# A fused attention and feed-forward kernel: maxima over partitions on TensorE, another order for the first units, less elementwise work on GpSimd

## The chip, the cores and the metric

The kernel runs on one core of one Trainium2 chip. The metric is device time in microseconds (us), as the median of several executions; lower is better.

## The reference

```python
scores = q @ k.T / sqrt(64)                      # batch 8, heads 8, sequence 576, head size 64
mask   = 0 <= rel < 32                           # heads 0 to 3: a plain window
         0 <= rel < 128 and rel % 4 == 0         # heads 4 to 7: a dilated window
attn   = softmax(where(mask, scores, -1e9))
x      = (attn @ v), heads side by side          # 4608 tokens x 512
h      = x @ w_in                                # 512 x 2048
g      = h * tanh(softplus(h))                   # Mish
out    = g @ w_out                               # 2048 x 512
```

q, k and v are float32. The two weight matrices are float64 (they come to the chip as 64-bit words), and the output is float32.

## The kernel before

The 4608 tokens are cut into 16 units of 288 tokens, two for each batch element. A unit goes through these steps, and the program names them by two letters: `ld` and `lv` load q, k and v; `pr` finds the largest magnitudes and makes power-of-two scales; `sc` computes a head's scores on TensorE and reduces them on DVE (VectorE); `ex` takes the exponential on ACT (ScalarE); `tp` transposes the probabilities; `va` multiplies by the values and normalises; `tx` transposes a pair of heads to x and splits it into a high and a low float16 half; `ff` is one of 16 blocks of the first product (twelve matmuls, L603) with Mish on ACT (L608); `gt` splits the result into two halves (ACT L623, then DVE L625, or POOL for the pairs in `ON_POOL`; POOL is GpSimd); `fo` is one of 16 blocks of the second product (L635), whose output is scaled (L642) and stored. A name such as `ff1.8` is unit 1, block 8; `sc0.7` is unit 0, head 7; `fo1.2.3` is unit 1, output block 2, part 3.

A feed-forward of one unit is 384 matmuls of 128 x 128 by 288 float16 columns: three products stand for one in higher precision, so each weight and each x is kept as a high and a low half. The first four units (`DIRECT`) compute attention in float32 straight from the loaded tensors. Units 4 to 15 split q, k, v and the probabilities in float16 halves and transpose the probabilities by DMA.

The weights are prepared on the chip while the first units run. There are two matrices (k = 0, 1), four column groups (g) and two parts (p), so 16 parts of 1 MB. A part goes through `wl` (load), `wm` (largest magnitude on DVE, L168, and a copy on ACT, L204), `ws` (the scale of a group, over both parts), `ww` (the float64 words turned into a float32, on DVE, L246, L247 and in some cases L249) and `wp` (scaled and split into two float16 halves). How a part is split is in the table `WAYS`: the first letter says whether the scaling is done through a sign and scale word on DVE (L260) with a product on POOL (L265), "S", or by ACT (L262), "A"; the second whether the low half is subtracted on POOL ("P") or DVE ("D") (L269). ACT makes the high half (L267).

The scale needs a maximum over the 128 partitions. That is `partition_all_reduce` on POOL: L210 for the eight weight groups, L336 for the 16 units.

For the first units the order of all instructions on every engine is written out in `ORDER`, a list of step names. A step is a generator; each time its name stands in the list it runs on to its next `yield`, so a step's pieces on different engines stand at different places. `kw` are matmuls on zeros. Engines run their own queues in this order, and SP (SyncE) issues all loads and stores in it. The list of before ends with the feed-forwards of units 0 and 1, attention of units 0 to 2 and the scores and exponentials of unit 3. What follows is sorted by due times (`at`, `heads`; 32 slots a unit), which fix TensorE's order alone. Loaded tensors share the tag `ld` with five buffers, raw weights have four buffers.

Softmax for heads in `BIASED` subtracts the maximum inside the exponential on ACT, one instruction for each block (L467); the others subtract on DVE (L452) and take one exponential.

Of the kernel before, what the change touches and what calls it, by code (L numbers as in the profile page):

```python
# [42 lines left out]
wp0.0.0 va0.3 sc1.0 kw5 va0.4 wm0.1.1 tx0.1 va0.5 ws0.1 wp0.0.0 va0.4 wl0.2.1 tx0.1 ww0.1.1 tp0.6 va0.5 tp0.6 ws0.1
wl0.2.0 va0.4 tx0.1 kw16 kw9 va0.6 va0.5 tp0.7 va0.6 ws0.1 tp0.7 tx0.2 sc1.2 va0.6 tx0.2 wp0.1.0 wp0.1.1 va0.7 sc1.6
tx0.2 wp0.1.0 fs0.1 sc1.4 sc1.2 va0.7 va0.7 wp0.1.1 kw4 sc1.5 wp0.1.0 sc1.6 tx0.3 tx0.3 sc1.4 kw4 sc1.1 wp0.1.0 tx0.3
kw2 sc1.3 sc1.5 ff0.0 sc1.1 wl0.3.1 ff0.3 ff0.0 sc1.3 lv1 wm0.2.0 ff0.1 ff0.3 wm0.2.1 wm0.2.0 ff0.4 lv2 ws0.2 ff0.1
ws0.2 ww0.2.0 wm0.2.1 ff0.6 ff0.4 ff0.5 ww0.2.1 ff0.6 wl0.3.0 ff0.2 ff0.5 ff0.7 ff0.2 wm0.3.1 gt0.0 sc1.7 ws0.2
# [728 lines left out]
```

## Time and profile before

| | |
|---|---|
| median of 3 runs | 1001.24 us (1000.7 to 1001.33) |
| the profiled execution: its own time | 1003.94 us |
| its span, first to last instruction | 1002.2 us |
| mean granted TensorE clock | 0.949 |
| TensorE busy, VectorE busy | 939.1 us, 674.8 us |
| ScalarE busy, GpSimd busy | 499.4 us, 86.0 us |

An engine's busy time is the sum of its instructions. The granted clock is the share of full speed that the clock of TensorE was given: at half of it a matmul takes twice as long. Most groups of instructions are given by line, engine, operation and the names of the tiles, with their count, busy time and mean duration in ns; behind the last bar stands how long the engine had been idle just before them and what ended that idle time.

### The profile page before, as it was taken

What the parts mean: (1) busy time and instruction counts of PE and PEld (TensorE: products, weight loads), DVE (VectorE), ACT (ScalarE), POOL (GpSimd) and SP (SyncE); (2) the same over time, 40 slices, a digit from 0 to 9 for tenths busy, and PEclk for the clock granted to TensorE, in tenths of its full rate; (3) what the DMA queues carried; (4) which work ended last, traced back from release to release, by engine and by line L of the source; (5) the groups of instructions that cost most, each with busy time, mean ns of one, the idle gap of its engine ahead of it and who ended that gap; (6) DMA issues with size and microseconds to landing.
All of it is one profiled execution on the core that took longest, in us unless ns stands there. A gap on an engine that the chain in (4) does not pass through costs nothing.

```text
span 1002.2 us, 21764 instructions
## 1 busy us (share of the span) xinstructions
PE 939.1 (94%) x8826; PEld 765.1 (76%) x8826; DVE 674.8 (67%) x1417; ACT 499.4 (50%) x926; POOL 86.0 (9%) x142
## 2 busy tenths in 40 slices
...
POOL 1320217142000000000000000000000000000000
PEclk6758597989999999999999999999999999999999
...
GB/s 278 29 115 105 121 96 84 219 12 97 146 129 155 81 145 67 157 35 173 49 159 75 136 87 115 126 88 140 67 174 52 113 13 141 8 56 20 18 7 24
DMA packets 138757, 98.02 MB, mean 98 GB/s; under 512 B 96033, under 2 KB 125345, under 8 KB 138657
## 3 DMA queue, kind: packets, MB, share of 16 engines
...
q8 instruction: 69, 1.13, 0.5%
q14 instruction: 32, 0.25, 0.1%
...
## 4 chain that ended last, share of the span: by engine, by line
PE 70%; DVE 13%; issue 6%; DMA 5%; POOL 2%; SPq 2%; ACT 2%; DVEq 0%; ACTq 0%; POOLq 0%
PE ph L603 31%; PE po L635 29%; DMA pT<-p 4%; PE psc L436 3%; PE pav L542 3%; PE psc L430 1%; PE px L568 1%; DVE raw L247 1%; DVE raw L260 1%; PE pav L536 1%; DVE am L168 1%; DVE m L168 1%; DVE nm L450 1%; DVE g L625 1%; DVE sb L452 1%
## 5 line engine op out<-in xcount | busy, mean ns | idle before, releaser
L603 PE MATMUL ph<-x,w 128*128 128x288 f16 x3072 | 408.4, 288 | 2.7 <-ACT w L204 1.1
L635 PE MATMUL po<-g,w 128*128 128x288 f16 x3072 | 393.3, 288 | 5.8 <-POOL w L269 5.8
L635 PEld LDWEIGHTS <-w 128*128 128x128 f16 x3072 | 297.7, 98 | 81.3 <-POOL w L269 6.0
L603 PEld LDWEIGHTS <-w 128*128 128x128 f16 x3072 | 295.2, 99 | 76.6 <-DVE w L246 2.0
L608 ACT ACTIVATE hm<-ph,fs 128x288 f32<-128x288 f32 x256 | 127.4, 499 | 219.0 <-PE ph L603 218.6
L625 DVE SCALAR_TENSOR_TENSOR g<-hm,sg,g 128x1152 f16<-128x1152 f32 x61 | 87.9, 1441 | 42.4 <-ACT g L623 42.4
...
L508 DVE TENSOR_TENSOR p<-sb,p 96x352 f16<-96x352 f32 (+3 forms) x96 | 48.4, 524 | 55.5 <-ACT p L506 55.4
L623 ACT ACTIVATE g<-hm,sg 128x1152 f16<-128x1152 f32 x61 | 76.3, 1251 | 0.6
L642 DVE TENSOR_SCALAR y<-po,fo 128x288 f32<-128x288 f32 x64 | 32.7, 511 | 48.0 <-PE po L635 47.6
L556 DVE TENSOR_TENSOR xs<-pav,rec 96x192 f32<-96x192 f32 (+1 forms) x128 | 49.4, 386 | 11.1 <-PE ptp L515 0.5
L452 DVE TENSOR_TENSOR sb<-sb,nm 96x256 f32<-96x256 f32 (+3 forms) x120 | 52.4, 449 | 1.1
L450 DVE TENSOR_REDUCE nm<-sb 96x2 f32<-96x256 f32 (+3 forms) x120 | 51.0, 441 | 1.2
L436 PE MATMUL psc<-ks,qs 128*96 128x128 f16 (+3 forms) x672 | 47.0, 211 | 4.9 <-DVE sb L444 2.8
L473 ACT ACTIVATE sb<-sb,ln_p 96x352 f32<-96x352 f32 (+3 forms) x96 | 49.1, 581 | 0.1
L436 PEld LDWEIGHTS <-qs 128*72 128x72 f16 (+1 forms) x672 | 42.7, 119 | 7.0 <-issue 5.2
L542 PEld LDWEIGHTS <-pT 128*128 128x128 f16 (+3 forms) x1008 | 43.1, 98 | 5.8 <-issue 1.4
L582 DVE TENSOR_TENSOR x<-px,x 128x288 f16<-128x288 f32 x48 | 30.0, 625 | 16.0 <-ACT x L580 16.0
L168 DVE TENSOR_REDUCE m<-vn 128x1 f32<-128x768 f32 x16 | 15.2, 949 | 32.3 <-DMA vn<-in_v 23.9
L515 PE MATMUL ptp<-ident,sb 96*128 96x96 f32 (+3 forms) x112 | 15.4, 273 | 19.8 <-ACT sb L472 16.6
L444 DVE SCALAR_TENSOR_TENSOR sb<-psc,sc,m_g 96x384 f32<-96x384 f32 (+1 forms) x48 | 29.7, 619 | 4.2 <-PE psc L436 4.2
L568 PE MATMUL px<-ident,xs 72*128 72x72 f32 (+1 forms) x224 | 28.4, 245 | 3.7 <-DVE xs L556 3.5
...
## 6 DMA issues: line engine op xcount, KB each, us to landing
...
```

The lines of the kernel that those rows point to most:

```text
L436: nc.tensor.matmul(pt[:nq, col:col + nk], d["qs"][:, h, pair, q0:q0 + nq], d["ks"][i][:, h, k0:k0 + nk], start=(i == 0), stop=(i == 1))
L450: nc.vector.tensor_reduce(nm[:nq, j:j + n], x, axis=AX.X, op=ALU.max, negate=True)
L452: nc.vector.tensor_tensor(o, x, nm[:nq, j:j + n].unsqueeze(2).broadcast_to([nq, n, w]), op=ALU.add)
L473: return [nc.scalar.activation(x, x, AF.Exp, bias=ln_p[:nq])]
L508: nc.vector.tensor_tensor(lo, src, hi, op=ALU.subtract)
L542: nc.tensor.matmul(avv[:, j], pp[:nk, c:c + P], vv[vi][:nk, j, head % 4, :], start=(i == 0), stop=(i == 2))
L556: nc.vector.tensor_tensor(xs[:nq, :nb, (head % 2) * D:(head % 2 + 1) * D], avv[:, :, :D], rc.unsqueeze(2).broadcast_to([nq, nb, D]), op=AL ...
L603: nc.tensor.matmul(ph[:, :HT], w1[:, c, j, wi, k * P:(k + 1) * P], d["x"][xi][:, c, :], start=(n == 0), stop=(n == len(seq) - 1))
L608: in_turn("mish", [nc.scalar.activation(d["m"][j][:, k], ph[:, :HT], AF.Mish, scale=d["fs"][:, j:j + 1])])
L623: nc.scalar.activation(g[:, 0], m, AF.Identity, scale=sg)
L625: nc.vector.scalar_tensor_tensor(g[:, 1], m, sg, g[:, 0], ALU.mult, ALU.subtract)
L635: nc.tensor.matmul(po[:, :HT], w2[:, e, j, wi, k * P:(k + 1) * P], d["g"][j][:, gi, k, :], start=(j == 0 and n == 0), stop=(j == NCH - 1 a ...
```

## The change

1. The maxima over partitions of the weights and of units 0 to 3 are made by a transpose on TensorE into PSUM, a reduction on DVE, and a product of a matrix of ones with the diagonal of the result, which brings it to all partitions (`over_partitions`). Units 4 to 15 keep the POOL instruction.
2. Eleven parts of the weights go a new way "AD": ACT writes the scaled high half directly from the float32 values, and DVE makes the low half with one scaled subtraction. Three parts stay "SP", two are "AP".
3. For ten pairs (`ON_PE`) the low half of x is made by a TensorE product with minus the identity onto the transposed x in PSUM, and ACT copies it out. Units 0 to 3 no longer scale x by v's scale at that place; the scale goes into the softmax denominator.
4. 19 heads instead of 6 are `BIASED`; four outputs (`ON_ACT`) are scaled on ACT; other pairs are in `ON_POOL`.
5. `ORDER` is new. It has 728 entries where there were 560, and holds the feed-forwards of units 0, 2 and 1 in this order, all attention of units 0 to 3, and preparation, scores and exponentials of unit 4. The due times start with unit 3. Weights of group 1 are loaded first.
6. Loaded tensors have a buffer each (`lA` to `lE`).

The new list, and then the core of the rest of the diff:

```
wl0.1.0 wl0.1.1 ld0 lv0 wl0.3.1 wl0.3.0 wm0.1.0 wm0.1.0 ww0.1.0 wm0.1.1 ws0.1 wm0.1.1 kw16 kw16 kw16 kw16 kw16 kw16
kw5 ws0.1 ws0.1 kw4 ws0.1 ww0.1.1 kw8 sc0.4 sc0.2 sc0.3 sc0.4 sc0.2 ex0.4 sc0.3 ex0.2 pr0 ex0.3 ws0.1 kw16 kw16 kw2
sc0.6 wp0.1.0 wm0.3.1 sc0.1 wp0.1.1 sc0.6 sc0.5 sc0.1 sc0.0 ex0.6 sc0.5 wp0.1.0 ex0.1 kw5 sc0.7 sc0.0 wl0.0.1 ex0.5
kw2 pr0 sc0.7 pr0 ex0.0 wm0.3.0 kw7 tp0.2 pr0 tp0.2 pr0 kw4 tp0.0 ex0.7 ws0.3 fs0.1 wp0.1.1 tp0.0 kw11 va0.2 wm0.3.1
ws0.3 va0.0 ws0.3 tp0.1 wl0.0.0 ws0.3 va0.2 ws0.3 va0.0 ld2 tp0.1 va0.2 wm0.3.0 va0.0 lv2 kw11 va0.1 fs0.3 tp0.4 va0.1
tp0.3 ww0.3.0 tp0.4 tp0.3 kw7 va0.3 va0.3 va0.1 wp0.3.0 va0.3 kw15 tx0.0 ww0.3.1 tx0.1 tx0.0 va0.4 tx0.1 tx0.0 tp0.7
va0.4 tx0.1 tx0.0 tx0.1 kw3 tp0.6 tp0.7 tp0.6 va0.4 wp0.3.1 kw7 va0.6 wp0.3.0 va0.7 tp0.5 va0.7 va0.6 wp0.3.1 tp0.5
sc2.2 va0.6 wl0.2.0 sc2.2 kw6 va0.5 wl0.2.1 va0.5 va0.7 ex2.2 va0.5 kw7 tx0.3 sc2.3 pr2 tx0.3 tx0.2 sc2.1 tx0.2 tx0.3
sc2.3 tx0.2 tx0.3 sc2.1 tx0.2 kw6 sc2.7 wm0.0.1 ex2.1 ff0.4 sc2.7 ex2.3 ff0.6 wm0.2.0 ex2.7 ff0.4 wm0.0.0 sc2.6 sc2.5
sc2.6 wm0.2.0 sc2.0 ws0.0 sc2.5 wm0.2.1 sc2.4 ff0.6 ex2.5 ff0.5 sc2.0 sc2.4 ff0.7 ws0.2 ww0.2.0 wm0.2.1 ff0.12 ex2.0
ff0.13 ex2.6 ww0.2.1 ex2.4 tp2.0 pr2 tp2.1 tp2.0 ws0.2 tp2.1 ws0.0 pr2 ff0.5 ws0.2 pr2 ws0.0 ws0.2 pr2 ws0.0 ws0.2
ff0.7 va2.0 va2.1 wm0.0.1 ws0.0 tp2.3 fs0.2 ff0.14 va2.0 fs0.0 wp0.2.1 va2.0 tp2.2 fs2 ff0.15 wp0.2.0 ww0.0.1 gt0.1
va2.1 tp2.3 wp0.2.1 tp2.2 ff0.12 va2.2 wm0.0.0 wp0.2.0 va2.2 ff0.13 gt0.1 ff0.8 ff0.14 ff0.15 va2.2 wp0.0.1 ff0.10
va2.1 ww0.0.0 gt0.3 tx2.0 va2.3 ff0.11 tx2.0 va2.3 ff0.8 ff0.10 tp2.4 tp2.6 tx2.0 ff0.11 ff0.9 va2.3 tp2.4 tp2.6 gt0.3
wp0.0.0 tx2.1 va2.4 va2.6 wp0.0.1 tx2.1 tp2.5 va2.4 tx2.1 va2.6 tp2.5 va2.4 wl1.1.0 tx2.1 va2.6 ff0.9 va2.5 wp0.0.0
gt0.2 tp2.7 va2.5 wl1.1.1 ff0.0 tp2.7 gt0.2 wl1.0.0 va2.7 va2.5 ff0.0 lv1 ff0.1 va2.7 va2.7 tx2.2 ff0.1 tx2.3 ld1
ff0.3 tx2.2 wm1.1.0 tx2.3 wl1.0.1 tx2.2 ff0.2 tx2.2 tx2.3 wm1.1.0 ff2.0 ff0.3 ww1.1.0 ff0.2 ff2.1 ff2.0 gt0.0 ff2.2
ff2.1 wm1.1.1 gt0.0 ff2.4 ff2.2 wm1.1.1 ff2.5 ff2.4 wm1.0.0 ff2.6 ff2.5 wm1.0.0 ff2.7 ff2.6 pr1 ff2.3 ff2.7 gt2.1
ws1.1 ff2.3 gt0.0 ws1.1 pr1 gt2.0 ws1.1 pr1 ws1.1 pr1 pr1 wp1.1.0 gt2.1 ff2.8 fs1 gt2.1 sc1.3 ff2.8 ff2.10 sc1.3
ww1.1.1 ex1.3 ff2.9 sc1.1 ff2.10 ff2.11 gt2.0 wp1.1.1 sc1.2 sc1.1 ff2.12 sc1.2 ff2.15 wp1.1.0 ff2.9 ff2.11 ff2.12
ff2.14 wm1.0.1 wp1.1.1 gt2.2 sc1.0 ff2.15 ff2.14 gt2.2 sc1.4 ex1.2 sc1.7 sc1.0 ff2.13 ex1.1 sc1.4 wm1.0.1 tp1.2 sc1.7
ex1.0 sc1.5 tp1.2 ww1.0.1 ex1.4 tp1.0 fo2.1.0 ex1.7 sc1.5 tp1.0 fo2.1.1 ff2.13 ww1.0.0 sc1.6 ex1.5 va1.0 ld3 va1.2
ws1.0 fo2.1.2 lv3 gt2.3 sc1.6 fo0.1.0 va1.0 ws1.0 va1.2 gt2.3 ex1.6 va1.0 wl1.2.0 va1.2 tp1.1 tp1.3 gt2.3 wl1.2.1
tp1.1 ws1.0 fo0.1.1 tp1.3 ws1.0 va1.3 wp1.0.0 va1.1 wp1.0.1 fo2.1.3 va1.3 wp1.0.1 va1.1 va1.3 tp1.6 fo2.1.3 va1.1
sc3.4 tp1.6 sc3.2 wp1.0.0 wp1.0.1 sc3.6 sc3.4 wp1.0.1 sc3.3 sc3.2 ex3.4 fo2.0.0 sc3.6 ex3.2 tp1.5 tx1.0 sc3.3 tp1.5
tx1.1 ex3.6 fo2.0.1 pr3 ex3.3 fo2.0.2 tx1.0 tx1.1 wm1.2.0 va1.6 tx1.1 va1.6 tp1.4 tx1.1 tx1.0 va1.6 fo2.0.3 wm1.2.0
tp1.4 fo0.1.2 ww1.2.0 tx1.0 fo2.0.3 va1.4 va1.5 va1.4 sc3.7 va1.5 tp1.7 va1.4 fo0.0.0 tp1.7 sc3.7 sc3.0 va1.5 ex3.7
wm1.2.1 va1.7 sc3.1 va1.7 sc3.0 wm1.2.1 sc3.5 va1.7 fo0.0.1 ex3.0 lv4 sc3.1 ws1.2 sc3.5 tx1.2 ex3.1 tx1.3 tx1.2
fo0.0.2 wl1.3.1 ws1.2 ww1.2.1 ex3.5 wl1.3.0 tx1.3 ws1.2 tx1.2 tp3.4 fo0.0.3 tx1.2 ws1.2 tp3.4 fo0.1.3 fo0.0.3 tx1.3
wp1.2.0 wp1.2.1 ff1.0 fo0.1.3 wp1.2.1 tp3.0 ff1.4 ff1.0 wp1.2.0 wm1.3.1 ff1.7 ff1.4 tp3.0 wp1.2.1 ff1.1 ff1.7 wp1.2.1
ff1.2 wm1.3.1 ff1.1 wm1.3.0 ff1.3 ff1.2 ww1.3.1 wm1.3.0 ws1.3 ff1.6 ff1.3 ws1.3 ff1.5 ff1.6 ww1.3.0 ws1.3 ff1.12 ff1.5
ff1.13 ff1.12 ws1.3 ff1.14 wp1.3.1 ff1.13 wp1.3.0 wp1.3.1 pr3 ff1.15 pr3 ff1.14 pr3 wp1.3.0 fo2.2.0 ff1.15 wp1.3.1 pr3
fo2.2.1 wp1.3.1 va3.0 va3.4 va3.0 fo2.2.2 va3.4 va3.0 ol ld4 va3.4 tp3.1 tp3.3 tp3.1 fo2.2.3 tp3.3 va3.1 fo2.2.3
fo0.3.0 va3.1 va3.1 tx3.0 tp3.2 tx3.0 fo2.3.0 tp3.2 tx3.0 va3.2 va3.3 va3.2 pr4 fo2.3.1 va3.3 tp3.6 tp3.5 tp3.6
fo2.3.2 tp3.5 fo2.3.3 va3.2 fo0.2.0 pr4 fo2.3.3 va3.3 va3.5 fo0.2.1 va3.5 va3.5 tx3.1 tx3.2 tx3.1 fo0.2.2 tx3.2 tx3.1
va3.6 tx3.2 fo0.2.3 va3.6 va3.6 tp3.7 fo0.2.3 fo0.3.1 tp3.7 pr4 va3.7 gt1.0 fo0.3.2 pr4 gt1.0 fo0.3.3 ff1.8 fo0.3.3
ff1.11 gt1.1 pr4 ff1.10 va3.7 gt1.3 fo1.3.0 ff1.8 ff1.11 ff1.10 gt1.1 ff1.9 pr4 va3.7 fo1.2.0 gt1.3 ff1.9 gt1.2 tx3.3
fo1.3.1 pr4 tx3.3 fo1.2.1 gt1.2 tx3.3 fo1.0.0 tx3.3 sc4.0 sc4.1 sc4.0 sc4.2 sc4.3 fo1.0.1 sc4.1 sc4.4 fo1.2.2 sc4.2
sc4.5 fo1.0.2 sc4.3 sc4.6 sc4.4 fo1.0.3 sc4.7 sc4.5 fo1.3.2 sc4.6 fo1.3.3 fo1.2.3 fo1.3.3 sc4.7 fo1.1.0 fo1.0.3 ex4.0
fo1.2.3 fo1.1.1 ex4.1 fo1.1.2 ex4.2 ex4.3 ex4.4 fo1.1.3 ex4.5 ex4.6 ex4.7 fo1.1.3
```

```diff
 WAYS = {
-    (0, 0, 0): "SP", (0, 0, 1): "SP", (0, 1, 0): "SP", (0, 1, 1): "AP", (0, 2, 0): "SD", (0, 2, 1): "AD", (0,
-    3, 0): "AP", (0, 3, 1): "AD", (1, 0, 0): "SP", (1, 0, 1): "SD", (1, 1, 0): "SD", (1, 1, 1): "SP", (1, 2,
-    0): "AP", (1, 2, 1): "AP", (1, 3, 0): "SD", (1, 3, 1): "SP",
+    (0, 0, 0): "AD", (0, 0, 1): "AD", (0, 1, 0): "AD", (0, 1, 1): "AD", (0, 2, 0): "AD", (0, 2, 1): "AD", (0,
+    3, 0): "AD", (0, 3, 1): "AD", (1, 0, 0): "AD", (1, 0, 1): "SP", (1, 1, 0): "AD", (1, 1, 1): "AP", (1, 2,
+    0): "AP", (1, 2, 1): "SP", (1, 3, 0): "AD", (1, 3, 1): "SP",
 }
-ON_POOL = {(0, 2), (1, 0), (1, 1)}
-BIASED = {(0, 0), (0, 1), (0, 2), (0, 4), (0, 6), (0, 7)}
+ON_POOL = {(0, 0), (2, 1), (2, 3)}
+BIASED = {(0, 0), (0, 1), (0, 2), (0, 3), (0, 4), (0, 5), (0, 6), (0, 7), (1, 3), (1, 7), (2, 0), (2, 1), (2, 2),
+    (2, 3), (2, 4), (2, 5), (2, 6), (3, 3), (3, 4)}
+ON_PE = {(0, 0), (0, 1), (0, 2), (0, 3), (1, 0), (1, 1), (1, 2), (2, 1), (2, 2), (3, 3)}
+ON_ACT = {(0, 0), (1, 3), (2, 0), (2, 1)}
...
+    ones = const.tile([4, 1], F32, name="ones")
+    nc.vector.memset(ones, 1.0)
+
+    def over_partitions(m, n):
+
+        pm = ps.tile([P, 512], F32, tag="a", name="pm", bufs=4)
+        nc.tensor.transpose(pm[:n, :P], m, ident)
+        yield
+        c = small.tile([4, 1], F32, name="c", bufs=4)
+        nc.vector.tensor_reduce(c[:n], pm[:n, :P], axis=AX.X, op=ALU.max)
+        if n > 1:
+            dg = small.tile([4, 4], F32, name="dg", bufs=2)
+            nc.vector.tensor_scalar(dg[:n, :n], ident[:n, :n], c[:n], None, ALU.mult)
+        yield
+        o = pm[:, 256:256 + n]
+        nc.tensor.matmul(o, ones[:n].broadcast_to([n, P]), dg[:n, :n] if n > 1 else c[:n], start=True, stop=True)
+        yield
+        return o
...
+        o = yield from over_partitions(am, n)
         mr = early.tile([P, n], F32, name=f"wr{n}", bufs=4)
-        nc.gpsimd.partition_all_reduce(mr, am, P, bass_isa.ReduceOp.absmax)
-        yield
-        nc.vector.tensor_scalar(mr, mr, TINY_HI, HI, ALU.max, ALU.mult)
+        nc.vector.tensor_scalar(mr, o, TINY_HI, HI, ALU.max, ALU.mult)
...
+                nc.scalar.activation(halves(d, 0) if way == "AD" else v, v, AF.Identity, scale=sc)
+        if way == "AD":
+            yield
+            for v, _, d, sc in parts:
+                nc.vector.scalar_tensor_tensor(halves(d, 1), v, sc, halves(d, 0), ALU.mult, ALU.subtract)
+            return
...
+            o = yield from over_partitions(m[:, 0:1], 1)
+            m3 = pool.tile([P, 3], F32, name="m3", bufs=3)
+            nc.vector.tensor_copy(m3[:, :1], o)
+            pow2_scales(m3[:, :1], f[:, :1], s[:, :1])
+            eps = d["eps"] = pool.tile([P, 1], F32, name="eps", bufs=4)
+            nc.vector.tensor_scalar(eps, f[:, :1], EPS, None, ALU.mult)
...
+            if (u, pair) in ON_PE:
+                nc.tensor.matmul(px[:, q0:q0 + nq], xs[:nq, j], ident[:nq, :nq], is_transpose=True, start=(i == 0),
...
+        nc.scalar.copy(hi, src)
+        yield
+        if (u, pair) in ON_PE:
+            nc.tensor.matmul(src, minus, hi, start=False, stop=True, skip_group_check=True)
+            yield
+            nc.scalar.copy(lo, src)
...
+            if (u, e) in ON_ACT:
+                nc.scalar.activation(y, po[:, :HT], AF.Identity, scale=fo)
...
-    heads(3, None, None, (64.2, 1.2), (65.7, 1.2), (67.5, 1.2))
+            heads(u, None, None, (T - 26, 1.9), (T - 20.6, 1.9), (T - 17, 1.9))      # unit 4
-        heads(u, (T - 54, 1) if u == 4 else (T - 62, 2), T - 46, (T - 45, 2.2), (T - 40, 2.2), (T - 36, 2.2))
+        heads(u, (T - 62, 2) if u > FIRST + 2 else (T - 50, 1.5), T - 46 if u > FIRST + 2 else T - 38, (T - 45, 2.2) if u > FIRST + 2 else (T - 37, 2.2), (T - 40, 2.2) if u > FIRST + 2 else (T - 32, 2.2),
+              (T - 36, 2.2) if u > FIRST + 2 else (T - 28, 2.2))
```

More of the change, by code (lines that the diff above doesn't have):

```diff
@@ L43 @@
[L43 to L47, printed above, removed]
@@ L121, in attn_mish_ffn_kernel @@
     pool = ctx.enter_context(tc.tile_pool(name="pool", bufs=1))
+    small = ctx.enter_context(tc.tile_pool(name="small", bufs=1))
     early = tc.alloc_tile_pool(name="early", bufs=1)
@@ L255, in w_split @@
         x, dst, s = lo.bitcast(F32), w_dst(k, g, p), ready[k, g]
-        for c in range(1 if k == 0 else WIDE):
-            v, h = (x, hi) if k == 0 else (x[:, c], hi[:, c])
-            sc = s[p * WIDE + c]
+        parts = [(x, hi, dst, s[0])] if k == 0 else [(x[:, c], hi[:, c], dst[:, c], s[p * WIDE + c]) for c in range(WIDE)]
+        halves = lambda d, i: d[:, :, i] if k == 0 else d[:, i]
+        for v, h, d, sc in parts:
             if way[0] == "S":
@@ L286, in loads @@
         kw, kd = d["kw"], d["kd"]
-        qn = d["qn"] = pool.tile([P, 4, HT], F32, tag="ld", name="qn", bufs=LD)
+        tq, tk = ("lE", "lD") if d["direct"] and half else ("lA", "lC")
+        qn = d["qn"] = pool.tile([P, 4, HT], F32, tag=tq, name="qn")
         nc.sync.dma_start(qn, qT[b, half])
-        knp = pool.tile([P, 2 * kw], F32, tag="ld", name="knp", bufs=LD)
+        knp = pool.tile([P, 2 * kw], F32, tag="lB", name="knp")
         nc.sync.dma_start(knp.rearrange("p (a k) -> p a k", a=2), kT[b, :, :, k0:k0 + kw])
-        knd = pool.tile([P, 2 * NR * kd], F32, tag="ld", name="knd", bufs=LD)
+        knd = pool.tile([P, 2 * NR * kd], F32, tag=tk, name="knd")
         for a in range(2):
@@ L328, in prep @@
         amax(m[:kd, 1:2], vdn[:kd])
-        if not d["direct"]:
-            qn, kn = d["qn"], d["kn"]
-            for i, x in enumerate(kn):
-                amax(m[:, 2 + i:3 + i], x)
-            amax(m[:, 4:5], qn)
+        qn, kn = d["qn"], d["kn"]
+        for i, x in enumerate(kn):
+            amax(m[:, 2 + i:3 + i], x)
+        amax(m[:, 4:5], qn)
         yield
-        mr = pool.tile([P, 5], F32, name="mru", bufs=3)
+        mr = pool.tile([P, 5], F32, name="mru", bufs=2)
         nc.gpsimd.partition_all_reduce(mr, m, P, bass_isa.ReduceOp.absmax)
@@ L377, in prep @@
             nc.gpsimd.memset(vdh[i][:, :, :, D:D + 1], one)
+        yield
+        both = []
         for src, dst, n in ((vn, vh, P), (vdn, vdh, kd)):
```

106 lines of the change are left out of this document (42 added, 64 removed).

## The prediction

> **What bounds the kernel now.** I read the page first, then the busy time by stretch, then the chain of waits and the list of waits over the first 310 us.
>
> ```profile
> PE 939.1 (94%) x8826; PEld 765.1 (76%) x8826; DVE 674.8 (67%) x1417; ACT 499.4 (50%) x926; POOL 86.0 (9%) x142
> POOL 1320217142000000000000000000000000000000
> PEclk6758597989999999999999999999999999999999
> ```
>
> TensorE is the bound over the span, but POOL's work and the low clock both lie in the first ten slices (250 us). The next view has, for each stretch, its length and then the busy time of PE, PEld, DVE, ACT and POOL, PE's granted clock, the DMA share and GB/s.
>
> ```profile
> 0.00:73.00 73.00, 54.05 (x404) 44.81 (x405) 38.70 (x93) 25.74 (x61) 18.23 (x31) 0.66 0.41 134
> 73.00:247.40 174.40, 141.53 (x1102) 110.26 (x1102) 131.77 (x251) 89.82 (x149) 51.98 (x49) 0.86 0.35 106
> 308.00:451.00 143.00, 137.76 (x1386) 112.79 (x1385) 113.20 (x235) 77.38 (x142) 4.47 (x18) 0.99 0.51 105
> 451.00:877.80 426.80, 426.26 (x4309) 351.53 (x4307) 311.48 (x673) 233.47 (x436) 9.05 (x37) 1.00 0.46 101
> ```
>
> From 451 us on PE hardly stops: 451 and 877.8 are the same point of two units, so eight units take 53.35 us each, and nothing in this change reaches them. The loss is in the first 247.4 us: PE idles 51.8 us there, at 0.66 and then 0.86 of its clock. TensorE's own timeline gives the milestones: first feed-forward of unit 0, its second half, unit 1's, the end of the hand-written order, and the end of unit 2's feed-forward.
>
> ```profile
> 72.95 7.07 PE L603 MATMUL ph<-x,w 128*128 128x288 f16 x37
> 116.80 0.69 PE L603 MATMUL ph<-x,w 128*128 128x288 f16 x2
> 137.67 16.53 PE L603 MATMUL ph<-x,w 128*128 128x288 f16 x132
> 247.43 1.63 PE L603 MATMUL ph<-x,w 128*128 128x288 f16 x12
> 308.03 1.63 PE L603 MATMUL ph<-x,w 128*128 128x288 f16 x12
> ```
>
> What holds it up is in the chain (start, length, what), where "issue" is time in which the engine waited for nothing that the profile shows, and in the waits (total, times, longest):
>
> ```profile
> 11.41 8.18 issue
> 54.75 4.70 issue
> 103.96 7.64 issue
> 155.02 7.29 DVE raw L260 x6
> 179.60 4.79 issue
> ```
>
> ```profile
> ACT w L267 <- POOL raw L265: 26.6, 6, 8.7
> PE ptp L515 <- ACT sb L472: 16.6, 2, 15.9
> DVE m L339 <- POOL mru L336: 9.0, 2, 8.7
> DVE wr L212 <- POOL wr L210: 7.7, 2, 5.2
> DVE w L246 <- PE ph L603: 7.4, 2, 4.8
> PE psc L426 <- DVE sb L452: 7.1, 1, 7.1
> PE po L635 <- POOL w L269: 5.8, 1, 5.8
> ```
>
> Each long "issue" step ends in a POOL all-reduce or a POOL product after one. The reader should see that the 0.41 us of the instruction is not its price; its row in POOL's timeline shows 9.64 us before it:
>
> ```profile
> 19.59 0.41 POOL L336 PARTITION_ALL_REDUCE mru<-m  x1 [9.64 <-issue]
> ```
>
> The 15.9 us hole at 90 to 107 us is ACT's queue standing behind L267, which waits 8.7 us for POOL's product, with unit 1's exponentials queued after it. The 7.1 us hole at 159 us is DVE: six L260 take 7.29 us while POOL multiplies.
>
> **The change, part by part.** Durations (busy total, mean ns):
>
> ```profile
> L168 DVE TENSOR_REDUCE am<-raw 128x1 f32<-128x1024 f32 x8 | 9.6, 1210 | 0.0
> L246 DVE TENSOR_SCALAR w<-w 128x1024 int32<-128x1024 int32 x16 | 11.7, 733 | 11.3 <-PE ph L603 7.4 <-ACT w L204 3.9
> L247 DVE SCALAR_TENSOR_TENSOR raw<-raw,w 128x1024 int32<-128x1024 int32 x16 | 19.6, 1227 | 0.5
> L249 DVE SCALAR_TENSOR_TENSOR raw<-raw 128x1024 int32<-128x1024 int32 x6 | 9.2, 1527 | 0.2
> L262 ACT ACTIVATE raw<-raw,s 128x1024 f32<-128x1024 f32 x4 | 5.0, 1252 | 4.3 <-DVE s L225 4.2
> L265 POOL TENSOR_TENSOR raw<-raw 128x1024 f32<-128x1024 f32 x10 | 20.6, 2060 | 36.5 <-issue 14.6 <-DVE w L246 7.5 <-DVE nm L450 6.9
> L269 POOL TENSOR_TENSOR w<-raw,w 128x1024 f16<-128x1024 f32 x10 | 22.0, 2206 | 14.2 <-ACT w L267 7.1 <-DVE x L578 7.1
> L450 DVE TENSOR_REDUCE nm<-psc 72x4 f32<-72x288 f32 x8 | 3.6, 447 | 0.5 <-PE psc L430 0.5
> L556 DVE TENSOR_TENSOR xs<-pav,rec 72x256 f32<-72x256 f32 x64 | 26.9, 420 | 6.9 <-PE ptp L515 0.5 <-DVE rec L554 0.5
> L578 DVE SCALAR_TENSOR_TENSOR x<-px,s,x 128x288 f16<-128x288 f32 x16 | 10.9, 684 | 4.4 <-ACT x L576 4.3
> L625 DVE SCALAR_TENSOR_TENSOR g<-hm,sg,g 128x1152 f16<-128x1152 f32 x61 | 87.9, 1441 | 42.4 <-ACT g L623 42.4
> L430 PE MATMUL psc<-knp,qn 64*96 64x128 f32 x80 | 16.6, 350 | 0.4 <-DMA knp<-in_kT 0.4
> ```
>
> Maxima: twelve all-reduces leave POOL (eight of the weights, four of units 0 to 3). Each becomes a transpose and a product on PE (one matmul of 128 float32 columns at most 0.35 us as L430's, the second smaller) and two DVE reads; I take 0.25 + 0.20 us of PE and 0.25 to 0.41 us of DVE (L450 takes 0.447 us for more elements). Twelve trips are 5 us of PE and 4 us of DVE. The wait of each round trip is unknown: below it can't gain more than nothing, above it is 4.8 us, the longest that DVE waits for a PE busy with feed-forwards.
>
> Weights: eleven of sixteen parts now go ACT then DVE, with no POOL. An undisturbed DVE product is L247's 1.227 us (L249's 1.527 has one of 3 us beside POOL in it), so such a part is 1.21 + 0.73 + 1.23 + 1.23 + 1.23 = 5.6 us of DVE and 1.15 + 1.25 us of ACT. By my count of all sixteen, DVE gains some 9 us of weight work, POOL's falls from 42.6 to 17 us. Biased heads go from 6 to 19: 13 times 0.3 us less on DVE, 0.5 us more on ACT. Ten of sixteen transposes of x subtract on PE: 10 x 0.68 off DVE, 0.13 us each on PE. Four outputs go to ACT. These three roughly repay the 9 + 4 us. ACT has 149 us of work up to the end of the new order and isn't the bound. The moved loads and SP's new order I cost at nothing inside the order: the two weights of group 1 come first, before the queries, and raw buffers come free at the rate at which DVE splits them.
>
> The new order holds three feed-forwards, all attention of units 0 to 3 and unit 4's scores. Before reaches that at 308.0 less 1.4 (four value steps and a transpose of unit 4 more): 306.6 us. Now the new order by stage; each count is of steps in its list.
>
> Up to ff0.4: DVE has 5 maxima (6.0), 4 word steps of 3.19 (12.7), 4 splits (5.0), 11 score steps of 0.75 (8.2), 8 value steps of 0.17 + 0.38 (4.4), unit 0's maxima and scales (5.8) and small ones (3.1): 45 us. PE has 35. DVE begins its word steps only when ACT has made the masks (10.5 us) and one copy (1.15): 10.4 us idle. 10.4 + 45 = 56 without another wait; before is 73. I take 61, nearer to the low end since before's 34 us of DVE idle in this stretch are its start and the POOL waits quoted.
>
> ff0.4 to ff0.0: DVE 36.3 us (3 maxima, 4 word steps and 4 splits are 21.3; scores, values, two gates and scales 15), PE 29. The like stretch before (72.95 to 116.80) took 43.85 us for 34.2 of DVE work counted the same way, a factor of 1.28, or 1.09 without its 6.75 us wait behind L267. Between them 1.18: 43. Then four ff of 1.47 and some: 7.
>
> From ff2.0 to the end PE leads: 80 steps of twelve matmuls at 1.47 us are 117.6, 16 score steps 17.4, unit 4's 2.4, values, transposes and maxima 17: 154.5 us at full clock, against DVE's 117. Before, 137.67 to 247.43 held 91.3 us of such work (48 steps, 13 scores, the rest) in 109.8: 1.20. But 7.1 and 5.8 us of it are the two PE waits above and 4.6 the low clock after them (36 and 48 matmuls, below, at 0.176 us and not 0.1225), which leaves 1.01. POOL still has about 28 us of elementwise work in the new stretch, so I take the middle, 1.10: 170.
>
> ```profile
> 168.22 8.56 PE L635 MATMUL po<-g,w 128*128 128x288 f16 x48
> 203.93 6.32 PE L635 MATMUL po<-g,w 128*128 128x288 f16 x36 [5.82 <-POOL w L269]
> ```
>
> The step's 1.47 us at full clock stands in the chain:
>
> ```profile
> 247.59 1.47 PE ph L603 x12
> ```
>
> Sum: 61 + 43 + 7 + 170 = 281 us, against 306.6: 25.6 us gained. After it, unit 5's loads stand in SP's queue behind the order's last output, and its scores only some 26 us of PE work later; unit 4's took 26.5 us from their all-reduce to the first score before. I cost that wait at 4 us of a possible 0 to 12. Net 21.6 us. The profiled execution has a span of 1002.2 us and its own time is 1003.94, 2.7 above the median 1001.24; taken off the median: 979.6, say 980.
>
> The row says that the all-reduce costs its 9.64 us of waiting, not 0.41. The Trainium skill, GPSIMD Engine Reference, section 4.1 Engine selection, gives GpSimd for a reduction along the partition dimension; by that rule a 0.41 us instruction is exchanged for 0.8 us on two fuller engines, twelve of them would cost 5 us, and the sum would be 1006.
>
> **The rivals.** (1) All POOL waits close: 56 + 36.3 x 1.09 + 7 + 156 = 258.6, no later wait: 48 us less, 953; with half of it, 965. For it speaks that nearly all of before's holes end in POOL; against, that DVE would be 87% full from its start to ff0.0 (0.15). (2) DVE binds: each stage runs at before's factor with POOL (1.28, 1.20) after 63 us: 63 + 46.5 + 8 + 185 = 302.5, 4 us less, and no later wait: 997 (0.15). (3) Slower: a trip's two handoffs. DVE stands in its queue for PE, whose product stands behind feed-forwards waiting for weights that DVE makes. At 4.8 us a trip twelve cost 58; from 1.8 us a trip (21.6 / 12) the gain is gone; at 3 us, 36: 1016. For it, the 7.4 us of DVE <- PE; against, that steps for other units stand between the pieces (0.13). By the skill's rule above the kernel is slower too, in this way. (4) The all-reduce was hidden, only the list is different: then the two lists are worth the same, 1001 (0.05). Against it, the four issue steps on the chain.
>
> **How the numbers follow.** My forecast, 968 to 992, has 0.52; the rivals 0.15, 0.15, 0.13, 0.05. A change under 0.2% (2 us) can't be told from none. Faster: 0.52 + 0.15 + 0.15 of the cases less a little of (2): 0.80; same 0.06; slower 0.14. The range leaves out the extreme half of (1) and most of (3): 958 to 1002.
>
> **What would show it.** Right: no all-reduce before unit 4's; first ff of unit 0 at 56 to 66 us; the end of the order at 270 to 292; PE's waits in it without any for POOL over 3 us; DVE some 78% busy to ff0.0. Wrong: DVE waiting for the two products over 1.8 us a trip; ACT behind the biased exponentials and eleven table changes instead of seven; or PE waiting over 12 us for unit 5's scores.

## The result, and the profile after

The changed kernel takes 977.15 us (median of 4, 975.26 to 977.98) where the kernel before takes 1001.08 us (median of 4). The ratio is 0.976, with a 95% interval of 0.974 to 0.978: 24 us less. Executions that took over 1.5% more than the fastest of the same kernel (three of e1's ten below, and one of the kernel before) are left out of medians and ratios. The profiled execution of the changed kernel took 977.98 us; its span is 976.2 us and its mean granted clock 0.979 (0.949 before).

From the page of the changed kernel: busy time of the engines, then GpSimd's share and TensorE's granted clock over the span in 40 slices.

```profile
PE 935.6 (96%) x8924; PEld 761.1 (78%) x8924; DVE 671.2 (69%) x1428; ACT 514.3 (53%) x974; POOL 49.7 (5%) x114
POOL 1000123230000000000000000000000000000000
PEclk7988989999999999999999999999999999999999
```

VectorE has hardly less work (671.2 against 674.8 us) and ScalarE more; only GpSimd's fell much, by 36 us. What changed is when the work is done. TensorE's timeline shows the milestones of the prediction: the first feed-forward step of unit 0 (ff0.4), its step ff0.0, the end of the written order, which here is unit 3's first step, and unit 4's first step.

```profile
55.38 4.96 PE L661 MATMUL ph<-x,w 128*128 128x288 f16 x24
100.03 2.99 PE L661 MATMUL ph<-x,w 128*128 128x288 f16 x12 [1.19 <-DVE w L297]
273.35 6.05 PE L661 MATMUL ph<-x,w 128*128 128x288 f16 x48 [0.33 <-ACT y L701]
332.95 3.10 PE L661 MATMUL ph<-x,w 128*128 128x288 f16 x24
```

The point that the order reaches at 273.35 us was reached at 306.6 us before, so 33 us are gained. The next view, busy time by stretch, has the columns of the prediction (length; busy PE, PEld, DVE, ACT, POOL; granted clock; DMA share; GB/s). First the changed kernel:

```profile
0.00:55.40 55.40, 44.35 (x444) 37.84 (x445) 42.04 (x99) 29.39 (x77) 3.78 (x20) 0.85 0.70 220
55.40:100.00 44.60, 34.73 (x271) 26.38 (x270) 33.68 (x73) 31.32 (x66) 0.00 (x0) 0.88 0.17 55
0.00:273.30 273.30, 247.80 (x2140) 198.52 (x2141) 204.65 (x435) 155.53 (x304) 37.21 (x57) 0.93 0.42 123
273.30:976.20 702.90, 687.82 (x6784) 562.61 (x6783) 466.54 (x994) 358.78 (x670) 12.51 (x57) 1.00 0.43 92
```

and the kernel before, over the same work:

```profile
0.00:306.60 306.60, 252.51 (x2070) 202.35 (x2071) 215.36 (x442) 148.21 (x276) 72.24 (x85) 0.84 0.41 119
306.60:1002.20 695.60, 686.62 (x6761) 562.71 (x6757) 459.40 (x975) 351.18 (x652) 13.72 (x57) 1.00 0.41 88
```

In the first rows TensorE is busy as long as before (247.8 against 252.5 us) in 33.3 us less, and its clock is 0.93 instead of 0.84. In the last rows the same remaining work takes 702.9 us instead of 695.6: 7.3 us are given back. Net 26.0 us of span. How much is given back differs between executions: in the trace of e12, the changed kernel again, the order ends at 273.11 us and the rest takes 699.4 us, 3.8 more than before.

The chain after is 73% PE, 11% DVE, 8% DMA, 4% ACT and 2% issue (6% before), and 0% GpSimd (2% before). Its first all-reduce now stands where nobody waits for it, in GpSimd's timeline:

```profile
222.93 0.41 POOL L387 PARTITION_ALL_REDUCE mru<-m  x1 [7.20 <-DVE rec L609]
```

and the waits of TensorE and VectorE up to 150 and 273 us (total, times, longest) show what the new trips over TensorE cost:

```profile
PE ph L661 <- DVE w L297: 6.2, 2, 5.0
PE pm L190 <- DVE wm L253: 4.9, 1, 4.9
PE pm L199 <- DVE c L193: 3.2, 3, 2.3
DVE c L193 <- PE pm L190: 6.4, 3, 3.9
DVE wr L244 <- PE pm L199: 2.1, 3, 1.4
```

VectorE waits 6.4 us in all for twelve transposes, in three places, and 2.1 us for the products after them, about 0.7 us a trip; TensorE's 4.9 us before the first trip stand behind products of zeros only.

### The profile page after: what moved, and what is told of

Its sections match the earlier page's. It is cut to its first block, busy times and chain, and to the rows that moved or that the text cites. A ratio compares the mean times of both kernels' runs of the same rounds, so it can differ in the third digit from the quotient of the medians.

```text
span 976.2 us, 21949 instructions
## 1 busy us (share of the span) xinstructions
PE 935.6 (96%) x8924; PEld 761.1 (78%) x8924; DVE 671.2 (69%) x1428; ACT 514.3 (53%) x974; POOL 49.7 (5%) x114
## 4 chain that ended last, share of the span: by engine, by line
PE 73%; DVE 11%; DMA 8%; ACT 4%; issue 2%; SPq 2%; POOL 0%; DVEq 0%; ACTq 0%
PE ph L661 34%; PE po L693 27%; DMA pT<-p 3%; PE psc L482 3%; PE psc L488 3%; PE pav L594 2%; DMA knp<-in_kT 1%; DVE m L182 1%; PE px L627 1%; ACT sb L525 1%; PE pav L588 1%; DVE w L297 1%; DMA vn<-in_v 1%; DVE nm L502 1%; DVE raw L278 1%
## 5 line engine op out<-in xcount | busy, mean ns | idle before, releaser
L703 DVE TENSOR_SCALAR y<-po,fo 128x288 f32<-128x288 f32 x60 | 30.5, 511 | 47.3 <-PE po L693 46.0
L641 DVE TENSOR_TENSOR x<-px,x 128x288 f16<-128x288 f32 x54 | 33.8, 626 | 21.5 <-ACT x L634 21.5
L634 ACT CAST x<-px 128x288 f16<-128x288 f32 x64 | 37.6, 595 | 16.9 <-PE px L627 15.8
L496 DVE SCALAR_TENSOR_TENSOR sb<-psc,sc,m_f 96x352 f32<-96x352 f32 (+1 forms) x48 | 25.9, 539 | 9.2 <-PE psc L488 9.2
L609 DVE RECIPROCAL rec<-den 96x3 f32<-96x3 f32 (+1 forms) x128 | 21.5, 168 | 15.6 <-ACT den L603 9.6
```

What stands on the lines that cost most here:

```text
L496: nc.vector.scalar_tensor_tensor(shaped(sb), shaped(pt), d["sc"][:nq], masks[0], ALU.mult, ALU.add)
```

## The experiments

The theory (A) was that GpSimd's maxima cost by the wait before them, and that the new order lets the other edits use the time. Later runs ask about the end of the order, about GpSimd itself, and about the granted clock. The kernel before, beside them, took 1001.8, 1002.9 and 1001.9 us in the three groups of runs (e1 to e4, e5 to e8, e9 to e12).

### e1: the changed kernel with the maxima back on GpSimd

```diff
-        nc.tensor.transpose(pm[:n, :P], m, ident)
-        ... (reduction, product)
+        o = small.tile([P, 4], F32, name="mo", bufs=6)
+        nc.gpsimd.partition_all_reduce(o[:, :n], m, P, bass_isa.ReduceOp.absmax)
```

> The changed kernel with its twelve early maxima back on POOL's all-reduce, at the places where the TensorE transposes stand; all else (new order, ways, heads) stays. Theory A, what POOL costs is each change between all-reduce and elementwise work (6 to 9.6 us before the first of a kind), not the all-reduce: the first six all-reduces follow one another with no elementwise work between them, so the first feed-forward of unit 0 still starts within 3 us of 55.4 us; from the first gate on POOL (112 us) on they alternate with gates and splits, some ten changes of 6 to 7 us, part of them exposed: 985 to 1000 us in all. Rival R, every all-reduce costs its 8 us by itself: first feed-forward 10 us or more later than 55.4, and over 1000 us in all. Rival N, the maxima were hidden anyway: within 2 us of 977.

Measured: 999.8 us (median of seven), ratio 0.998 (0.995 to 1.001): the whole gain is gone. Its ten executions lie between 992 and 1008 us, and the one that was traced took 1007.5. GpSimd's timeline:

```profile
66.52 0.69 POOL L190 PARTITION_ALL_REDUCE mo<-wm  x2 [13.85 <-DVE wm L246]
118.06 0.40 POOL L190 PARTITION_ALL_REDUCE mo<-am  x1 [6.04 <-issue]
125.43 2.36 POOL L671 TENSOR_TENSOR g<-hm,g 128x1152 f16<-128x1152 f32 x1 [6.98 <-issue]
```

Up to 110 us GpSimd has only all-reduces after the masks; behind the first they wait for their inputs alone, and the first feed-forward starts at 55.90 us, as early as in the changed kernel. So R falls, which asked for 10 us more there. From the first gate on GpSimd (110.72 us) the two kinds of work alternate, and GpSimd stands idle for 5.8 to 9.6 us at each change (22 us at one that also waits for its input). The two at 118.06 and 125.43 stand inside one gate, between its two instructions.

The time is at the upper end of A's range. From the first feed-forward to the end of the order (302.14 us) this trace takes 246.2 us, and that of the changed kernel 218.0. TensorE is idle for 22 us more in it, 10.2 of them in one wait for hm L659 behind ACT's queue, and busy for 6 us more, at a granted clock of 0.90 and not 0.95.

### e2, e3, e4: the two parts on the old order

e2 has the maxima on TensorE (names in the old list stand once or twice more, for the added pieces), e3 the table of ways of the changed kernel save for one part, (1, 2, 1), which keeps its old way, e4 both.

```diff
 # e2, e4
-        nc.gpsimd.partition_all_reduce(mr, am, P, bass_isa.ReduceOp.absmax)
-        yield
+        o = yield from over_partitions(am, n)
 # e3, e4
-    (0, 0, 0): "SP", (0, 0, 1): "SP", (0, 1, 0): "SP", (0, 1, 1): "AP", ...
+    (0, 0, 0): "AD", (0, 0, 1): "AD", (0, 1, 0): "AD", (0, 1, 1): "AD", ...
```

> The kernel before with only the maxima of the weights and of units 0 to 3 moved to TensorE (two or one more places for their pieces in the old order); POOL keeps all its elementwise work. Theory A: no all-reduce is left in the first 230 us, so no change of kind: the waits in front of POOL work go (the 8.2, 4.7, 7.6 and 4.8 us steps of the chain), DVE's slow products beside POOL stay: 978 to 988 us. Rival O, the gain of the change is its new order: 995 to 1001 us. Rival D, the trips cost DVE 3 us or more each: over 1001 us.

> The kernel before with only the new ways for the weights (eleven parts by ACT and DVE, three parts with a product on POOL becoming two; part (1,2,1) keeps its old way); old order, all-reduces and gates on POOL as before. Theory A: until the first gate on POOL, all-reduces follow one another with no elementwise work between, so first feed-forward of unit 0 at 60 to 65 us and not 73, and no 15.9 us hole at 90 us; after it changes of kind remain: 983 to 992 us. Rival R, each all-reduce costs 8 us by itself: first feed-forward at 70 us or later, 995 to 1005 us since DVE has 9 us more work.

> The kernel before with both: maxima on TensorE and the new ways; old order. Theory A with the order as second: 975 to 985 us, a few us above the changed kernel, since either part alone already takes the changes of kind away and the old order holds only two feed-forwards. Rival O: 990 to 1001 us, the new order makes the gain.

| | median | ratio to before | first feed-forward |
|---|---|---|---|
| before | 1001.8 us | | 72.95 us |
| e2, maxima | 984.2 us | 0.983 (0.982 to 0.985) | 59.84 us |
| e3, ways | 984.4 us | 0.983 (0.980 to 0.987) | 68.11 us |
| e4, both | 996.5 us | 0.994 (0.992 to 0.996) | 72.98 us |

The times of e2 and e3 came as A said, though e3's first feed-forward is later than the 60 to 65 us that A gave. e4 did not: both parts together give less than either, and the time lies in the range of O, which e2 had ruled out for the maxima alone. Busy time by stretch in e4:

```profile
40.00:60.00 20.00, 15.13 (x122) 13.74 (x120) 14.99 (x29) 6.56 (x12) 0.00 (x0) 0.59 0.32 106
60.00:73.00 13.00, 13.00 (x66) 9.63 (x65) 9.58 (x19) 3.76 (x5) 0.19 (x3) 0.50 0.63 152
```

and in e2:

```profile
40.00:60.00 20.00, 16.23 (x149) 13.39 (x148) 18.90 (x40) 10.43 (x16) 12.79 (x11) 0.83 0.37 122
```

e4's TensorE runs without a gap from 60 to 73 us, at half its clock. From 54 to 73 us that is up to 9.5 us more for the same products, of the 13.1 us that e4's first feed-forward is later than e2's. So the clock became a suspect of its own.

### e5: e4 with TensorE kept busy in its 4.3 us hole

```diff
-... kw5 va0.4 wm0.1.1 tx0.1 ...
+... kw5 va0.4 wm0.1.1 kw16 kw16 kw16 kw16 tx0.1 ...
```

> The kernel of e4 (old order with both new parts; 996.5 us, first feed-forward at 72.98) with 64 more products of zeros on TensorE, put where it idles 4.33 us (45.8 to 50.1, before px L597). Theory C, the granted clock: in e4 that idle time is followed by 0.50 of the clock from 48 to 77 us, so the scores and products up to the first feed-forward take twice their time; kept busy, TensorE holds 1.00, the first feed-forward starts at 62 to 67, and the time is 984 to 991. Theory D, the old order itself stands in the way of both parts together and the clock only follows: the first feed-forward stays at 71 to 75 and the time at 994 to 999.

Measured: 999.0 us, ratio 0.996 (0.994 to 0.998), first feed-forward at 72.44 us. TensorE's timeline:

```profile
44.19 3.74 PE L703 MATMUL pz<-zeros 128*128 128x128 bf16 x64
50.03 0.47 PE L597 MATMUL px<-ident,xs 96*128 96x96 f32 x3 [2.10 <-DVE xs L585]
```

The products ended too soon, 2.10 us of the hole were left, and the clock stayed at 0.50 from 52 to 72 us. Theory D fits the number, but what C asked for, no hole, was not reached: this run tells the two not apart.

### e6: the changed kernel with 24 products of zeros at 121 us

```diff
-... gt0.0 ws1.1 pr1 gt2.0 ws1.1 ...
+... gt0.0 ws1.1 pr1 kw24 gt2.0 ws1.1 ...
```

> The changed kernel with 24 more products of zeros on TensorE where it idles 1.45 us around 121 us (between the transposes L190 and the products L199). Theory C, the clock: in the changed kernel 124 to 131 us run at about 0.5 after these short gaps; kept at 1.00 they give 3 to 4 us, the order ends at 269 to 271 and the time is 973 to 975. Theory D, VectorE's work is what is waited for there and later: the clock's gain is waited away again, 976 to 979.

Busy time by stretch, the changed kernel:

```profile
120.00:136.00 16.00, 14.55 (x87) 10.00 (x85) 12.06 (x27) 11.68 (x17) 5.16 (x3) 0.79 0.00 0
```

and e6:

```profile
120.00:136.00 16.00, 15.89 (x139) 12.61 (x138) 11.16 (x27) 10.70 (x17) 4.67 (x3) 1.00 0.01 2
```

Here the hole was closed and the clock kept. Measured: 974.2 us, ratio 0.973 (0.969 to 0.977), in the range of C, but the interval overlaps that of the changed kernel, so the time does not show a gain. From the first feed-forward (59.38) to the end of the order (275.20) are 215.8 us in its trace, against 218.0 in the changed kernel: 2.2 us. That the products kept the clock is not shown either: e8's trace, below, kept it behind the same hole without them.

### e7: unit 5's preparation held back

```diff
-... pr4 tx3.3 ... ex4.7 fo1.1.3
+... pr4 ld5 lv5 tx3.3 ... ex4.7 fo1.1.3 pr5 pr5 pr5 pr5 pr5 pr5 pr5
-        at(T - 76, prep, u)
+        if u > FIRST + 2: at(T - 76, prep, u)
```

The loads are issued where they were (246.5 us); what is held back is the preparation.

> The changed kernel with unit 5's loads and preparation held behind unit 4's scores and exponentials at the end of the written order, so that its maxima and splits on VectorE no longer stand between unit 4's score steps. Theory A, these steps make TensorE's waits at 259 and 262 us (1.48 and 1.23 us behind sb L496): they go, first feed-forward of unit 3 at 270 to 272, time 973 to 976. Rival B, what I predicted: unit 5's scores are then late after the order, a wait of 4 to 12 us there: 980 to 987.

In the changed kernel's order, TensorE waits twice for VectorE, which does unit 5's maxima between unit 4's score steps:

```profile
259.15 0.44 PE L488 MATMUL psc<-ks,qs 128*72 128x72 f16 x8 [1.48 <-DVE sb L496]
262.29 0.44 PE L488 MATMUL psc<-ks,qs 128*72 128x72 f16 x8 [1.23 <-DVE sb L496]
```

In e7 these two are gone, and others stand behind the order:

```profile
269.75 6.04 PE L661 MATMUL ph<-x,w 128*128 128x288 f16 x48
284.38 6.04 PE L661 MATMUL ph<-x,w 128*128 128x288 f16 x48 [1.75 <-ACT hm L666]
313.56 0.53 PE L488 MATMUL psc<-ks,qs 128*72 128x104 f16 x8 [1.93 <-DVE x L641]
321.46 0.53 PE L594 MATMUL pav<-vdh,pT 72*128 72x65 f16 x12 [3.81 <-DVE sb L496]
```

First feed-forward to end of order: 269.75 - 57.51 = 212.2 us, against 273.35 - 55.38 = 218.0. Of these 5.8 us, 1.9 had been gained by 201 us, ahead of the edit, with another clock; the edit gives 3.8. End of order to unit 4's first step (334.32 in e7, 332.95 in the changed kernel): 64.6 against 59.6 us, 5.0 given back. The time is 977.0 us (ratio 0.974, 0.971 to 0.977), that of the changed kernel, and in the range of neither theory. A was right for the order and B, in its mechanism, for what follows it: the work for unit 5 that VectorE no longer does in the order is waited for behind it.

### e8: one output back on VectorE

```diff
-ON_ACT = {(0, 0), (1, 3), (2, 0), (2, 1)}
+ON_ACT = {(0, 0), (2, 0), (2, 1)}
```

> The changed kernel with one output of unit 1 (u 1, e 3) back on VectorE, so that ACT does not stand 5.27 us behind fo L698 with unit 4's exponentials in its queue. Theory A, ACT's queue delays what follows the order: unit 4's exponentials start 3 to 5 us earlier, the waits at 280 to 309 us (0.80, 1.28, 2.16) shrink, time 973 to 976. Rival B, TensorE has other work there and only 0.33 us hung on it: 976.5 to 978.

Measured: 978.4 us, ratio 0.975 (0.972 to 0.978), that of the changed kernel, so A falls. Unit 4's exponentials do start earlier (262.65 instead of 274.61 us), and nothing came of it but two more table loads (1.28 us each) on ACT. The trace shows something else. TensorE's list of instructions is that of the changed kernel, yet the first feed-forward starts at 64.92 us instead of 55.38. Busy time by stretch in e8:

```profile
26.00:40.00 14.00, 14.00 (x86) 11.78 (x86) 8.51 (x26) 7.60 (x26) 0.00 (x0) 0.51 0.29 86
```

and in the changed kernel:

```profile
26.00:40.00 14.00, 11.79 (x138) 10.21 (x138) 12.21 (x40) 10.02 (x34) 0.12 (x1) 1.00 0.54 180
```

The same list gets through 86 products or 138, with the clock at 0.51 or at 1.00. e7's trace, whose list is the same up to there as well, has 0.59, and its first feed-forward at 57.51 us.

Nor did e8's trace lose the clock behind the hole that e6 filled. TensorE's timeline and the stretch around the hole, in e8:

```profile
133.10 0.38 PE L199 MATMUL pm<-dg,ones 4*128 4x4 f32 x2 [1.45 <-DVE dg L196]
120.00:136.00 16.00, 14.55 (x119) 11.43 (x116) 11.41 (x16) 10.11 (x15) 7.17 (x4) 1.00 0.29 91
```

The hole is there, 1.45 us long as in the changed kernel, and the clock is 1.00 and not 0.79. So what a hole costs differs between executions of the same list, and a few us between two single traces do not show what an edit gives.

### e9: what GpSimd's work costs by itself

All-reduces (R), elementwise products (T) and memsets (M) of 4 columns behind the masks, for nobody.

```diff
+    for kind in "RRRRMRTTTTMTRTRT":
+        if kind == "R":
+            nc.gpsimd.partition_all_reduce(pb, pa, P, bass_isa.ReduceOp.absmax)
+        elif kind == "T":
+            nc.gpsimd.tensor_tensor(pa, pb, pb, op=ALU.mult)
+        else:
+            nc.gpsimd.memset(pa, 1.0)
```

> The changed kernel with extra work of 4 columns on GpSimd right behind the masks, for nobody: all-reduces (R), elementwise products (T) and memsets (M) in the order RRRR M R TTTT M T R T R T. Theory A, the change of kind costs: each R behind a T and each T behind an R (and the first R) begins 6 to 10 us after the instruction before it, the other R and T follow within 1 us, and M changes nothing; five changes behind the first, some 40 us in all. Rival, every all-reduce costs its 6 to 10 us of issue: each of the seven R has it, and no T.

GpSimd's timeline:

```profile
19.61 1.82 POOL L181 PARTITION_ALL_REDUCE w<-w  x4 [5.97 <-issue]
21.50 0.10 POOL L185 MEMSET w<- 128x4 f32 x1
21.69 0.38 POOL L181 PARTITION_ALL_REDUCE w<-w  x1
29.32 1.02 POOL L183 TENSOR_TENSOR w<-w 128x4 f32<-128x4 f32 x4 [7.25 <-issue]
37.59 0.40 POOL L181 PARTITION_ALL_REDUCE w<-w  x1 [6.82 <-issue]
48.16 2.53 POOL L183 TENSOR_TENSOR w<-w 128x4 f32<-128x4 f32 x1 [10.17 <-DVE rec L622]
59.81 0.40 POOL L181 PARTITION_ALL_REDUCE w<-w  x1 [9.06 <-DVE sb L517]
67.46 0.19 POOL L183 TENSOR_TENSOR w<-w 128x4 f32<-128x4 f32 x1 [7.18 <-issue]
```

As A said: four R take 1.82 us and four T 1.02, a memset between changes nothing, and every change of kind, in both directions, costs GpSimd 6.0 to 10.2 us. (No instruction here needs rec L622 or sb L517; the releaser named is only what came last.) The one execution took 978.2 us, as long as the changed kernel: 46 us of idle GpSimd cost nothing that this run shows.

### e11: the third part undone

```diff
-    (0, 0, 0): "AD", (0, 0, 1): "AD", ...       # eleven parts
+    (0, 0, 0): "AP", (0, 0, 1): "AP", ...
```

> The changed kernel with the third part undone: the eleven weight parts whose low half VectorE makes in one instruction go back to ACT's scaled copy and GpSimd's subtraction (GpSimd 11 x 2.2 us more, ACT 11 x 1.1 more, VectorE 11 x 1.3 less); the maxima stay on TensorE. Theory A, GpSimd costs by its changes of kind, and none is added before 223 us: 977 to 985. Rival, elementwise work on GpSimd costs by itself, on the way of each weight: 988 or more.

Measured: 982.9 us, ratio 0.981 (0.979 to 0.984), where e12 beside it has 976.0: 7 us. In the traces the first feed-forward starts at 63.42 us (55.19 in e12), and the order ends at 280.44 (273.11), so all of it is lost before the first feed-forward. TensorE's longest wait for GpSimd up to 150 us stands behind that, at 97.82 us, where e12 has one of 5.0 us for VectorE's half (w L297):

```profile
PE ph L661 <- POOL w L305: 6.0, 1, 6.0
```

No issue stands before GpSimd's subtractions, in line with e9: they wait for ACT's copies (L303), and one takes 2.28 us. That the time lies in A's range and not the rival's does not say what the 7 us are. The clock from 20 to 40 us is 0.67 in this trace and 0.88 in e12's, and e8 starts its first feed-forward as late with no instruction changed up to there; but all six executions are longer than every one of e12. Whether the subtraction on GpSimd delays the weights there, or moves TensorE's holes and so the clock, is open.

### e10 and e12: the clock alone

e12 is the changed kernel again. e10 is that kernel with 212 products of zeros in six holes of TensorE before 122 us.

```diff
-... kw16 kw5 ws0.1 ws0.1 ...
+... kw16 kw5 kw80 ws0.1 ws0.1 ...
 (and kw24 before tx0.3, kw24 after the first ws0.0 behind tp2.1, kw48 after the first
  va2.2, kw12 before the first ff0.0, kw24 behind the pr1 before gt2.0)
```

> The changed kernel with products of zeros (212 in all) in six places where TensorE idles before 122 us: 80 at the start, 24 around 48, 24 around 72, 48 around 82, 12 around 98.5 and 24 around 121 us. Theory C, the granted clock is a loss of its own: it stays near 1.00 up to 147 us (0.85 to 0.91 now), the first feed-forward of unit 0 starts at 51 to 54, the order ends 4 to 8 us earlier, time 969 to 973. Theory D, VectorE sets the pace there and the low clock is only its trace: the clock is near 1.00 as well, but the milestones stay and the time is 975 to 979, or above if the products delay what waits behind them.

> The changed kernel as it is, beside the others on one chip, so that differences of a few us can be read: 975 to 980.

e10: 967.2 us, ratio 0.964 (0.962 to 0.967), below the range of C. e12: 976.0 us, ratio 0.974 (0.971 to 0.977). The intervals lie apart, and the medians differ by 8.8 us. Busy time by stretch, e10:

```profile
55.00:100.00 45.00, 39.05 (x398) 32.15 (x396) 36.98 (x78) 33.27 (x71) 0.00 (x0) 1.00 0.30 88
100.00:147.00 47.00, 46.89 (x392) 36.97 (x390) 37.88 (x67) 36.12 (x59) 14.10 (x9) 1.00 0.30 88
```

and e12:

```profile
55.00:100.00 45.00, 35.15 (x275) 26.61 (x274) 33.92 (x73) 31.72 (x67) 0.00 (x0) 0.88 0.17 57
100.00:147.00 47.00, 45.55 (x332) 34.35 (x331) 33.90 (x57) 31.84 (x54) 9.42 (x7) 0.89 0.31 83
```

and e10's milestones in TensorE's timeline:

```profile
54.46 3.11 PE L661 MATMUL ph<-x,w 128*128 128x288 f16 x24
263.80 4.58 PE L661 MATMUL ph<-x,w 128*128 128x288 f16 x36 [0.33 <-ACT y L701]
```

The order ends 9.3 us earlier than e12's (273.11), close to the gain in time. VectorE gets more done in each stretch (36.98 against 33.92 us of busy time in 45 us), so it was not the pace that D takes it for: it had been waiting for products at half the clock, and TensorE's wait for the weights (w L297) fell from 6.2 to 1.7 us. C holds for the changed kernel from the first feed-forward on, and e10 beats both kernels. Ahead of it C was wrong: up to 55 us the clock is 0.88 (0.85 in e12) in spite of the products, and the first feed-forward starts at 54.46 us, hardly earlier.

## Why the prediction came out right, step by step

The forecast was 980 us and the measured time is 977.15 us. That they lie so near is in part luck. Two stages came out 5.6 and 5.5 us shorter than forecast, two others 1.7 and 1.8 us longer, and what follows the order cost 3.3 us more: the errors cancel in part. The granted clock, a loss of its own as e10 shows, entered only with 4.6 us in the factor of the last stage. By the steps:

- **Up to ff0.4:** 61 us predicted, 55.4 measured, below even the 56 of the sum without another wait, and so just below the 56 to 66 that were named as a sign. The start was mis-sized: VectorE began its word steps at 8.64 us and not behind 10.4 us of idle time, since ACT made the weight's copy ahead of the masks. VectorE is busy 42.0 of the 55.4 us (I counted 45), 76%; I had said some 78% to ff0.0, and it is 75.7 of 100 us.
- **ff0.4 to ff0.0:** 43 predicted, 44.65 measured, with 33.7 us of VectorE work and not 36.3. The factor that I took between 1.09 and 1.28 is 1.33 by that count. e10 shows what is in it: in the changed kernel the clock is 0.88 in this stretch, and with 1.00 in e10 the stretch takes 95.39 - 54.46 = 40.9 us.
- **Four ff, then the rest of the order:** 7 and 170 predicted; unit 2's first step starts near 108.8 us, so 8.8 and 164.5 us. The factor 1.10 on 154.5 us was 1.06. I took the middle between 1.01 and 1.20 because of GpSimd's work, and did not ask what the clock would do. Part of these 10 us over 154.5 is again the clock, which is 0.91 from 108.8 to 147 us; at 1.00 these 38.2 us would take up to 3.4 us less, by estimate from that figure.
- **The gain at the end of the order:** 25.6 predicted, 33.3 measured.
- **After it:** 4 us (0 to 12) predicted, 7.25 measured (3.8 in e12's trace). The size is in the range, but the step that failed is its mechanism. Unit 5's loads do not stand behind the order's last output: SP issues them at 246.85 us, within the order, its all-reduce runs at 260.3 us, and its scores come in time. What is late is VectorE. Unit 5's maxima and splits fill it between unit 4's score steps (2.7 us of waits of TensorE), and values and x of unit 4 come late behind the order (1.28, 2.16 and 0.94 us between 304 and 328 us). e7 showed no gain from another place: moved behind the order, this work was waited for there. So what is said above of the kernel, that SP issues all in the order of the list, is too strict: work of the later units is put into the order's gaps.
- **GpSimd's price:** that the 0.41 us of the all-reduce is not its price was right; e1 gives the gain of 24 us wholly back. But a maximum does not cost a wait of its own, which is what I wrote of the 9.64 us: what costs is the change between all-reduces and elementwise work (e9). The rule of the Trainium skill, GPSIMD Engine Reference, section 4.1, that a reduction along the partitions belongs on GpSimd, does not hold here: the measurement decides against it (ratio 0.998 in e1 against 0.976). Section 2.1 of the same page says that the first call to a freshly loaded library kernel pays about 6 us for code loading, with no instruction to be seen. The trace of e9 agrees with 5.97 us for the first all-reduce, and has 6.8 to 10.2 us at every later change too.
- **The rivals.** The slower one, two handoffs a trip, asked for 1.8 us a trip; VectorE waited about 0.7. That the all-reduce was hidden falls with e1 and e2. That VectorE binds falls with e10, whose VectorE does the same work in 9 us less. That all waits for GpSimd close (965 or 953) is half true: they did close, and the clock and the work behind the order took the rest; with the holes filled, e10 has 967. Half of that rival's 48 us would have been 977 and not 965, which lies halfway between my forecast and 953; so the measured time alone does not part this rival from the forecast.

By parts, on the changed order: without the maxima on TensorE some 23 us are lost (e1), without the new ways of the weights 7 us (e11, the cause open). On the old order the maxima give 17.6 and the ways 17.4 us, and both together 5.3 (e4). Why the two work against each other there is not settled: e4's trace has the clock at 0.50 from 54 to 77 us, and e5, which was to take that away, did not close the hole. From e4 to the changed kernel are some 18 us more by the ratios; they belong to the new order together with parts 3, 4 and 6, which no run takes apart, save for one output in e8.
